# Two output transfers from two engines, and spare matmuls in TensorE's waits, in a decode kernel

## The chip, the cores and the metric

The kernel runs on one core of a Trainium2 chip. The metric is the device time of one execution in microseconds (us), as the median of several; "span" is the time from the first to the last instruction in a profiled execution, about 1.8 us shorter than the device time of the same execution (988.4 us in one of 990.19). An "issue" is the instruction by which an engine starts a transfer, a "landing" the moment at which the trace records that the transfer has completed. The change concerns the last 15 us of a run of 990 us.

## The reference

One decode step of a transformer block for 4 sequences of one token: layer norm, attention of 32 heads over caches of 4096 keys and values of width 192, an output projection with residual, then layer norm, a gated feed-forward part and a second residual.

```python
h  = x + attention(layernorm(x), k_cache, v_cache, wq) @ wo      # x: [4, 1, 640]
n  = layernorm(h)
h2 = h + (silu(n @ w_gate) * (n @ w_up)) @ w_down                # [640,1536], [640,1536], [1536,640]
```

The two caches are 403 MB of bfloat16. All weights together are about 22 MB. The output is 4 rows of 640 bfloat16 numbers, 5 KB.

## The kernel before

The kernel streams the caches through SBUF, and sends the weights of the last part behind them on the same queue. These are the parts that the change touches (cuts marked with `# ...`). `op` and `dma` note an instruction for an engine with the ones that it must wait for.

```python
    wd_land = {}
    for lo, hi in ((0, 6), (6, 11), (11, CF)):          # CF = 12 columns of w_down, in three transfers
        t = dma("sp", lambda e, lo=lo, hi=hi: e.dma_start(wdsb[:, lo:hi, :], ...), sem(f"s_wd{lo}"), k_free)
        for c in range(lo, hi):
            wd_land[c] = t
    # ... attention, wo ...
    ln2 = layer_norm(psH[:, 0:DQ], [wo_done])
    for k, w in enumerate((wgsb, wusb)):                # gate, then up
        for c in range(CD):                             # CD = 5
            for n in range(4):                          # four column tiles at a time, 384 columns each
                a = op("pe", lambda e, ...: e.matmul(PB[k][32 * n:32 * n + 32, 0:FQ], lhsT=lnT[:, c, :], ...),
                       [ln2, wu_land[c] if k else wg_land, ...])
        # ... silu on ScalarE after gate
    # ... gate times up, and its transpose, on VectorE
    for c in range(CF):
        for n in range(4):                              # 160 columns each
            a = op("pe", lambda e, c=c, n=n: e.matmul(psH[32 * n:32 * n + 32, 0:DQ], lhsT=guT[:, c, :], ...),
                   [gut, wd_land[c], ln2])
    a = op("dve", lambda e: e.tensor_copy(out=outsb[:, 0:DQ], in_=psH[:, 0:DQ]), [a])
    fin = dma("act", lambda e: e.dma_start(
        out[:, 0, :].rearrange("b (n d) -> n b d", n=4), outsb[0:128:RB, 0:DQ]), S_out, [a])
```

A result row of sequence `b` lies in four quarters, on partitions `32n + 8b`, so the output transfer writes 16 rows of 320 bytes in a 4 by 4 pattern. Matmuls come in groups of four that run side by side on the four column tiles of the array (in the trace of before, the first four of w_down start within 0.01 us).

## Time and profile before

| | before |
|---|---|
| device time, median of the 6 runs timed beside the changed kernel | 990.52 us (990.11 to 990.92) |
| span of the profiled run | 988.4 us |
| HBM read | 424.29 MB, 429 GB/s over the span |
| last landing of w_down | 985.08 us |
| copy of the result starts | 985.79 us |
| output issued / complete | 986.14 / 987.90 us |

The page of the kernel before: the share of DMA in 40 equal slices of the span (tenths), and the chain of work that ended last, by engine and by line.

```profile
span 988.4 us, 9461 instructions
...
DMA  9999999999999999999999999999999999999997
...
DMA 67%; PE 18%; DVE 12%; issue 1%; SPq 1%; DVEq 0%
```

All slices but the last have DMA at nine tenths or more. The chain is DMA for two thirds; the VectorE and TensorE pieces in it are the work that sets cache buffers free for the next load (SyncE's issues of the value loads waited for TensorE 30 times, 836.7 us in all). The change leaves that part alone. What it can shorten is the tail behind the last bytes of w_down.

The timeline of the tail: start, duration, engine, line, what is written and read, how often; in brackets the idle time of the engine before it and what ended it.

```profile
975.92 1.79 PE L563 MATMUL pb<-wg_sb,lnT 128*32 128x384 bf16 x20 [1.90 <-DVE lnT L322]
...
978.60 1.15 PE L563 MATMUL pb<-wu_sb,lnT 128*32 128x384 bf16 x12 [0.88 <-DMA wu_sb<-in_B_w_up_dram]
...
980.48 0.83 PE L563 MATMUL pb<-wu_sb,lnT 128*32 128x384 bf16 x8 [0.73 <-DMA wu_sb<-in_B_w_up_dram]
...
982.93 0.99 PE L573 MATMUL pb<-wd_sb,guT 128*32 128x160 bf16 x24 [1.62 <-DVE guT L569]
...
984.75 0.99 PE L573 MATMUL pb<-wd_sb,guT 128*32 128x160 bf16 x24 [0.83 <-DMA wd_sb<-in_B_w_down_dram]
985.79 0.33 DVE L576 CAST gu<-pb 128x160 bf16<-128x160 f32 x1 [2.91 <-PE pb L573]
986.14 1.13 ACTq L577 DMA_DIRECT2D out_dram<-gu  x1
```

TensorE waits for w_up twice (0.88 and 0.73 us), for VectorE's transpose (1.62), and for the second chunk of w_down (0.83). The last 24 matmuls start at 984.75, and the copy can start 1.04 us later. The output's issue is one instruction of ScalarE, 1.13 us long.

The chain of waits in order of time gives the release of those 24 matmuls (start, duration, what):

```profile
946.58 38.12 DMA wd_sb<-in_B_w_down_dram
...
984.75 1.02 PE pb L573 x18
...
985.79 0.33 DVE gu L576
```

The last w_down chunk landed at 985.08, by the landings that the trace records, but the matmuls that need it came last in the row of 24, and were not held up by it.

The granted clock, by windows (busy time of TensorE first; then weight loads, VectorE, ScalarE, GpSimd; the granted share of full clock; DMA share; GB/s):

```profile
core 0: us, PE busy (x) PEld busy (x) DVE busy (x) ACT busy (x) POOL busy (x), PEclk, DMA share, GB/s
975.40:978.80 3.40, 1.99 (x24) 0.84 (x28) 0.44 (x2) 1.20 (x2) 0.00 (x0) 0.50 1.00 413
978.80:982.20 3.40, 1.78 (x20) 0.29 (x12) 0.73 (x2) 0.00 (x0) 0.00 (x0) 0.50 1.01 413
...
984.70:985.80 1.10, 0.99 (x24) 0.67 (x24) 0.01 (x1) 0.00 (x0) 0.00 (x0) 0.50 0.00 0
```

From 975.4 us on TensorE has half its clock (0.50).

### The profile page before, as it was taken

The page shows a single profiled execution, that of the slowest core. Times are in us where ns is not written, and L with a number is a line of the kernel's source. Part 1 is how long each engine was busy: PE and PEld are TensorE (multiplying, and loading weights), DVE is VectorE, ACT ScalarE, POOL GpSimd, SP SyncE. Part 2 cuts the span into 40 slices and gives each one's busy share as a digit, 9 for nine tenths or more (in the row PEclk, how much of TensorE's full clock was granted, in tenths as well). Part 3 has the DMA queues.
Part 4 walks back from the last instruction along what each step waited for, and adds up shares of the span by engine and source line. Part 5 has one row for each costly group of instructions (what it writes and reads, how often), then busy time and mean ns, then how long its engine had stood idle before and what let it go on. Part 6 is the DMA issues. An engine that isn't in the chain of part 4 may idle for free.

```text
span 988.4 us, 9461 instructions
## 1 busy us (share of the span) xinstructions
PE 580.1 (59%) x4409; PEld 129.6 (13%) x2941; DVE 552.5 (56%) x447; ACT 117.1 (12%) x376; POOL 3.6 (0%) x18
## 2 busy tenths in 40 slices
PE   1677555666555576555557755656665555765554
PEld 0011011110101111001111110111101011110023
DVE  1486555566645556664556665555666455566621
ACT  0311111110111110011111011111101111100120
POOL 1000000000000000000000000000000000000000
PEclk9898777887777888777788777788877778887775
DMA  9999999999999999999999999999999999999997
GB/s 403 426 440 432 430 438 424 440 430 434 438 424 442 430 432 438 424 442 430 434 436 426 440 434 430 438 426 438 434 430 438 426 438 434 430 438 426 438 431 325
DMA packets 10571, 424.39 MB, mean 429 GB/s; under 512 B 1220, under 2 KB 1348, under 8 KB 1732
## 3 DMA queue, kind: packets, MB, share of 16 engines
q1 hardware_dynamic: 10512, 424.28, 99.5%
q8 instruction: 5, 0.08, 0.0%
q10 hardware_dynamic: 52, 0.01, 0.0%
q14 instruction: 2, 0.02, 0.0%
HBM read 424.29 MB, written 0.01 MB: 429 GB/s over the span
## 4 chain that ended last, share of the span: by engine, by line
DMA 67%; PE 18%; DVE 12%; issue 1%; SPq 1%; DVEq 0%
DMA k<-in_A_k_cache_dram 63%; DVE prod L413 12%; PE pb L161 12%; PE pb L463 4%; DMA wd_sb<-in_B_w_down_dram 4%; PE pb L421 2%; SPq L366 0%; DVE sc L426 0%; PE pb L469 0%; DVEq L413 0%; PE pb L573 0%; SPq L386 0%; SPq L392 0%; PE pb L435 0%; SPq L331 0%
## 5 line engine op out<-in xcount | busy, mean ns | idle before, releaser
L413 DVE TENSOR_TENSOR prod<-k,qball 128x6144 f16<-128x6144 bf16 x128 | 426.3, 3352 | 220.7 <-DMA k<-in_A_k_cache_dram 220.7
L161 PE MATMUL pb<-prod,identH 128*128 128x512 f16 x1408 | 385.0, 430 | 0.0
L421 PE MATMUL pb<-prod,identH 128*128 128x512 f16 x128 | 57.9, 452 | 339.5 <-DVE prod L413 339.5
L426 DVE TENSOR_REDUCE sc<-pb 128x32 f32<-128x512 f32 x128 | 88.0, 688 | 107.6 <-PE pb L161 107.6
L478 ACT ACTIVATE otmp<-pb,minv 128x192 f32<-128x192 f32 x32 | 13.5, 421 | 650.8 <-PE pb L463 650.8
L421 PEld LDWEIGHTS pb<-prod,identH 128*128 128x128 f16 x128 | 13.2, 103 | 586.2 <-DVE prod L413 481.3
L463 PE MATMUL pb<-v,pbuf 128*8 128x384 bf16 x1984 | 86.0, 326 | 0.0
L454 ACT ACTIVATE pbuf<-sc,negM 32x128 bf16<-32x128 f32 x128 | 73.4, 574 | 4.9
L463 PEld LDWEIGHTS pb<-v,pbuf 128*8 128x8 bf16 x1984 | 45.4, 86 | 28.8
L482 DVE SCALAR_TENSOR_TENSOR orow<-pb,minv,otmp 128x192 f32<-128x192 f32 x32 | 13.4, 418 | 55.0 <-ACT otmp L478 55.0
L498 PEld LDWEIGHTS pb<-orow,here 128*128 128x128 f32 x256 | 33.5, 191 | 73.8 <-issue 71.1
L498 PE MATMUL pb<-orow,here 128*128 128x48 f32 x256 | 31.7, 267 | 1.1 <-DVE orow L482 1.1
L454 ACT ACTIVATION_READ_ACCUMULATOR pbuf<-sc,negM 32x1 f32 x128 | 31.8, 248 | 0.0
L448 ACT ACTIVATE negM<-pb 128x4 f32<-128x4 f32 x32 | 5.6, 174 | 160.9 <-PE pb L444 160.9
L469 PEld LDWEIGHTS pb<-lsb,headm 128*128 128x128 f32 x64 | 12.3, 194 | 74.8 <-issue 71.1
L444 PE MATMUL pb<-negMc,ones_row 1*128 1x4 f32 x64 | 12.2, 258 | 11.9 <-DVE negMc L439 11.9
L435 PE MATMUL pb<-identF,msb 128*1 128x128 f32 x64 | 12.1, 271 | 9.8 <-DVE msb L431 9.8
L439 DVE TENSOR_REDUCE negMc<-pb 1x4 f32<-1x128 f32 x32 | 8.9, 279 | 15.1 <-PE pb L435 15.1
L444 PEld LDWEIGHTS pb<-negMc,ones_row 1*128 1x128 f32 x64 | 9.4, 182 | 21.3 <-DVE negMc L439 21.3
L469 PE MATMUL pb<-lsb,headm 128*128 128x1 f32 x64 | 9.2, 213 | 2.7 <-ACT pbuf L454 2.7
L491 ACT ACTIVATE here<-place 128x131 f32 (+1 forms) x32 | 10.0, 312 | 0.9
L431 DVE TENSOR_REDUCE msb<-sc 128x1 f32<-128x128 f32 x32 | 9.2, 286 | 1.1
(65 smaller groups left out, 85.1 us busy)
## 6 DMA issues: line engine op xcount, KB each, us to landing
k<-in_A_k_cache_dram SPq DMA_DIRECT2D x32, 6144.0 KB, 39.5
v<-in_A_v_cache_dram SPq DMA_DIRECT2D x31, 6144.0 KB, 25.5
wq_sb<-in_A_wq_dram SPq DMA_DIRECT2D x1, 7680.0 KB, 21.4
k<-in_A_v_cache_dram SPq DMA_DIRECT2D x1, 6144.0 KB, 39.2
wo_sb<-in_A_wo_dram SPq DMA_DIRECT2D x1, 5760.0 KB, 24.9
wo_sb<-in_A_wo_dram SPq DMA_DIRECT2D x1, 1920.0 KB, 26.9
wg_sb<-in_B_w_gate_dram SPq DMA_DIRECT2D x1, 1920.0 KB, 31.1
wu_sb<-in_B_w_up_dram SPq DMA_DIRECT2D x1, 1152.0 KB, 33.4
```

The source lines that it names most:

```text
L161: return e.add_instruction(mybir.InstMatmult(name=e.bass.get_next_instruction_name(), engine=mybir.EngineType.PE, start_tensor_calc=start, ...
L413: op("dve", lambda e: e.tensor_tensor(out=prod[BUF[k]][:, :, :], in0=kslot[u % 2][:, k * QT:(k + 1) * QT, :], in1=qball[:, bass.ds(u + pr. ...
L421: op("pe", lambda e, j=j: (e.matmul if j == 0 else partial(held_matmul, e))(psR[k][:, 0:QT * R], lhsT=identH[:, :], rhs=prod[BUF[k]][:, :, ...
L426: op("dve", lambda e: e.tensor_reduce(sc[u % 2][:, k * QT:(k + 1) * QT], psR[k][:, 0:QT * R].rearrange("q (t r) -> q t r", r=R), AX.X, ALU ...
L435: op("pe", lambda e: e.matmul(psS[0:1, XT], lhsT=msb[:, 0:1], rhs=identF[:, :], start=True, stop=True), [g("rmax", u), g("negM", u - 1), p ...
L444: op("pe", lambda e: e.matmul(psS[:, XB], lhsT=ones_row[0:1, :], rhs=negMc[0:1, :], start=True, stop=True), [g("hmax", u), g("negM", u - 1 ...
L454: op("act", lambda e, h=h, r=r: e.activation(out=pbuf[r, :, h], in_=sc[u % 2][r, :], func=ACTF.Exp, bias=negM[r, h:h + 1], scale=alpha, ac ...
L463: op("pe", lambda e, t=t, n=n: e.matmul(psO[32 * n:32 * n + 8, 0:2 * DH], lhsT=pbuf[:, t:t + 2, :].rearrange("q t m -> q (t m)"), rhs=vsrc ...
L469: op("pe", lambda e: e.matmul(psS[:, XL], lhsT=headm[:, :, :].rearrange("q r m -> q (r m)"), rhs=lsb[:, :], start=True, stop=True), [g("ex ...
L478: op("act", lambda e: e.activation(out=otmp[:, :], in_=psO[:, 0:DH], func=ACTF.Copy, scale=minv[:, 0:1]), [g("pv", u), g("minv", u), g("st ...
L482: op("dve", lambda e: e.scalar_tensor_tensor(out=orow[:, :], in0=psO[:, DH:2 * DH], scalar=minv[:, 1:2], in1=otmp[:, :], op0=ALU.mult, op1 ...
L498: op("pe", lambda e, i=i: e.matmul(psT[:, bass.ds(JW * at_unit(u)[0], JW)], lhsT=here[:, NI - 1 - i:NI - 1 - i + 128], rhs=orow[:, JW * i: ...
```

## The change

Three things are done, with the same arithmetic. The output goes in two transfers of eight rows, one from SyncE and one from ScalarE, so that each has half of the rows. Fourteen matmuls whose result nobody reads fill the waits of the feed-forward part, so that the clock comes up to full. And w_down arrives as 6, 4 and 2 columns instead of 6, 5 and 1, so that fewer matmuls are left behind its second chunk.

```diff
-    for lo, hi in ((0, 6), (6, 11), (11, CF)):
+    for lo, hi in ((0, 6), (6, 10), (10, CF)):
 # ...
+    def idle(n):
+        for _ in range(n):
+            op("pe", lambda e: e.matmul(PB[2][:, 0:256], lhsT=sel[:, 0, :], rhs=sel[:, 0:2, :].rearrange("q b m -> q (b m)"),
+                                        start=True, stop=True), [tk["rsum", NU - 1, NQ - 1]])
     for k, w in enumerate((wgsb, wusb)):
         for c in range(CD):
+            if c == 3 and k == 1:
+                idle(2)
 # ... gate / up matmuls
+        idle(6 if k else 3)
 # ...
     for c in range(CF):
+        if c == 6:
+            idle(3)
 # ... w_down matmuls, copy
-    fin = dma("act", lambda e: e.dma_start(
-        out[:, 0, :].rearrange("b (n d) -> n b d", n=4),
-outsb[0:128:RB, 0:DQ]), S_out, [a])
+    fin = [dma(eng, lambda e, n=n: e.dma_start(
+        out[:, 0, n * DQ:(n + 2) * DQ].rearrange("b (n d) -> n b d", n=2),
+        outsb[32 * n:32 * n + 64:RB, 0:DQ]), S_out, [a]) for n, eng in ((0, "sp"), (2, "act"))]
 # ...
-        pr.emit(block, "act", [fin])
+        pr.emit(block, "act", fin[-1:])
```

Both transfers raise the same semaphore, and ScalarE waits at the end for the sum of both.

## The prediction

> **What bounds it now.** DMA. The page's slices show the DMA share at nine tenths or more in all but the last, about 430 GB/s; the chain that ended last is 67% DMA. In the tail it is still the w_down load until 984.70 us, then the second half of the w_down matmuls (1.02 us), the copy (0.33), and the output: its issue on ScalarE is one instruction of 1.13 us (986.14 to 987.27) for 16 rows; completion is recorded at 987.90, the span closes at 988.4. Only these last 3.7 us can change; what comes before is set by 424 MB of reads that the change leaves alone.

> **What the change does.**
> 1. *w_down split 6/5/1 columns becomes 6/4/2.* Same bytes, so the last chunk should still land at 985.08 (issue at 947.07 plus 38.0). Before, the second chunk landed at 984.70 and 24 matmuls ran behind it; the last four needed the third chunk only at 985.25, so it was hidden. Now the second chunk should land near 984.3 (estimate: one column takes 55 ns a row, eight rows an engine), its 16 matmuls finish in the wait, and 8 run after 985.08. Groups of four start 0.133 us apart, the tail after the last start is 0.37: the copy is released near 985.6 instead of 985.76. Gain 0.15 us.
> 2. *14 spare matmuls of 256 columns.* Each costs about 0.21 us at half clock (estimate, from 0.133 for 160 columns). They fit the waits: before w_up (0.88 us idle, 0.64 used), within it (0.73; 0.43), after it (1.62; 1.28), within w_down (0.83; 0.64). They serve only the clock. Its record changes on a grid of 3.413 us[...]. In this trace half clock turned to full after a window that matmuls filled to 0.79 or more (34 cases), never at 0.76 or less. In the feed-forward part the shares were 0.53, 0.39, 0.46: half clock to the end. With the spares I work out 0.73, then 0.86: full clock from about 982.2. The last 8 matmuls then cost about 0.15 us less (a matmul took 0.233 us at full clock at the end of wo, 0.341 here). Earlier matmuls wait for DMA anyway. Chance that the clock is up in time: 80%.
> 3. *Output in two transfers of 8 rows.* The 1.13 us issue compares with 0.33 (after a wait) for a plain 128-row load, so part of it goes by rows or outer dimension; I take 0.8 for each half (0.55 to 1.13). [...] The closing wait covers both. Gain 0.2 us net.

> **Sum.** 0.15 + 0.12 + 0.2, about 0.5 us of 990.47: **989.95 us**, range 989.3 to 990.6 (before's runs spread 0.4). Faster by over 2%: 0.002; within 2%: 0.996; slower: 0.002.

> **What would show it.** Landings: second w_down chunk near 984.3, last near 985.1. Windows: full clock after about 982; 8 matmuls after the last landing, done 0.4 to 0.5 us later. Timeline: two output issues near 985.8, each under 0.9 us.

> **What would make it wrong.** The two issues exclude each other (no gain, or 0.3 us loss); 8 rows cost the same 1.1 us; a grid that falls so that no window reaches 0.79; a spare matmul delaying a real one; or landings that shift by tenths from run to run and hide it.

The sum stands as 0.15 + 0.12 + 0.2, 0.47 us. That the two issues would run side by side, on which the 0.2 rests, was the assumption; no trace of before shows it.

## The result

| | before | changed |
|---|---|---|
| median of 6 runs | 990.52 us (990.11 to 990.92) | 990.44 us (990.08 to 990.74) |
| ratio, 95% interval | | 0.9999 (0.9986 to 1.0012) |
| span of the profiled run | 988.4 us | 988.3 us |

All these runs were fast, within 1.5% of the fastest run of the kernel. A ratio here is the mean time of one kernel's fast runs over that of the other's of the same rounds, so it is not quite the ratio of the medians. The time lies in the forecast range, but the forecast gain of 0.5 us does not show: the medians differ by 0.08 us, the six runs of the changed kernel spread over 0.66 us, and the interval of the ratio is about 1.3 us to either side, so that these times can neither show such a gain nor exclude it. One has to read the traces to see what the change did.

The page after, the lines that answer to those of before:

```profile
DMA  9999999999999999999999999999999999999997
...
DMA 67%; PE 18%; DVE 12%; issue 1%; SPq 1%; DVEq 0%
```

The bulk is the same. The timeline of the tail:

```profile
975.98 1.79 PE L570 MATMUL pb<-wg_sb,lnT 128*32 128x384 bf16 x20 [1.90 <-DVE lnT L322]
...
977.71 0.82 PE L562 MATMUL pb<-sel 128*128 128x256 bf16 x3
...
980.45 0.51 PE L570 MATMUL pb<-wu_sb,lnT 128*32 128x384 bf16 x8 [0.71 <-DMA wu_sb<-in_B_w_up_dram]
...
980.89 0.83 PE L562 MATMUL pb<-sel 128*128 128x256 bf16 x6
...
982.90 0.60 PE L583 MATMUL pb<-wd_sb,guT 128*32 128x160 bf16 x24 [1.18 <-DMA wd_sb<-in_B_w_down_dram]
...
984.36 0.46 PE L583 MATMUL pb<-wd_sb,guT 128*32 128x160 bf16 x16 [0.42 <-DMA wd_sb<-in_B_w_down_dram]
...
985.11 0.32 PE L583 MATMUL pb<-wd_sb,guT 128*32 128x160 bf16 x8 [0.29 <-DMA wd_sb<-in_B_w_down_dram]
985.48 0.33 DVE L586 CAST gu<-pb 128x160 bf16<-128x160 f32 x1 [2.96 <-PE pb L583]
985.84 0.68 SPq L587 DMA_DIRECT2D out_dram<-gu  x1
985.84 1.38 ACTq L587 DMA_DIRECT2D out_dram<-gu  x1
```

The lines with `pb<-sel` are the spare matmuls. None of them delays a real one here: the w_up and w_down matmuls behind them still wait for DMA or start with its landing. The 24 first matmuls of w_down took 0.60 us instead of 0.99, which is the clock. The second chunk now releases 16 matmuls at 984.36 and the third releases 8 at 985.11. The copy starts at 985.48, 0.30 us sooner than before. Both output issues start at 985.84. SyncE's takes 0.68 us and ScalarE's 1.38 us: longer than the one issue of all 16 rows (1.13).

The end of the chain in order of time:

```profile
947.14 37.92 DMA wd_sb<-in_B_w_down_dram
...
985.11 0.35 PE pb L583 x8
...
985.48 0.33 DVE gu L586
```

The clock by windows, as above:

```profile
975.40:978.80 3.40, 2.78 (x27) 1.13 (x31) 0.49 (x2) 1.25 (x2) 0.00 (x0) 0.52 1.01 420
978.80:982.20 3.40, 2.20 (x28) 0.90 (x20) 1.08 (x2) 0.00 (x0) 0.00 (x0) 0.98 1.00 408
...
984.70:985.80 1.10, 0.44 (x16) 0.12 (x8) 0.32 (x1) 0.00 (x0) 0.00 (x0) 1.00 0.00 0
```

Full clock from 979.0 on. The chain now goes through the last chunk of w_down, as forecast.

When the rows really move is not in the timeline, which shows only the issue. Windows of 0.1 us show it in their last two columns, DMA share and GB/s. Before:

```profile
987.30:987.40 0.10, 0.00 (x0) 0.00 (x0) 0.00 (x0) 0.00 (x0) 0.00 (x0) 0.50 0.00 0
987.40:987.50 0.10, 0.00 (x0) 0.00 (x0) 0.00 (x0) 0.00 (x0) 0.00 (x0) 0.50 0.15 38
987.50:987.60 0.10, 0.00 (x0) 0.00 (x0) 0.00 (x0) 0.00 (x0) 0.00 (x0) 0.50 0.07 13
```

And after:

```profile
987.10:987.20 0.10, 0.00 (x0) 0.00 (x0) 0.00 (x0) 0.00 (x0) 0.00 (x0) 0.50 0.11 26
987.20:987.30 0.10, 0.00 (x0) 0.00 (x0) 0.00 (x0) 0.00 (x0) 0.00 (x0) 0.50 0.00 0
987.30:987.40 0.10, 0.00 (x0) 0.00 (x0) 0.00 (x0) 0.00 (x0) 0.00 (x0) 0.50 0.04 10
987.40:987.50 0.10, 0.00 (x0) 0.00 (x0) 0.00 (x0) 0.00 (x0) 0.00 (x0) 0.50 0.07 16
```

Before, all rows move between 987.4 and 987.6. After, there are two bursts, with nothing in 987.2 to 987.3. The trace's DMA packets say it to the nanosecond: the first half's rows start at 987.111 us and its last packet at 987.184, the second half's start at 987.380. So the DMA engines stood idle for almost 0.2 us before the second half: it was not held up by the moving of the first half's rows.

The tail of every run below, from the trace's own records (us). "Copy" and "rows" are the starts of the copy and of the first row's packet, "complete" is the last semaphore step of the output, "end" the end of the span. Landings differ by some tenths between runs, so each row is counted from its own last landing of w_down:

```
run                    last landing   copy     issue to  issue to   copy to    landing
                       of w_down      after it rows      complete   complete   to end
before                 985.075        0.711    1.289     1.758      2.116      3.299
changed                985.064        0.419    1.540*    1.962*     2.319      3.209
e1_act_half            985.030        0.552    1.292     1.718      2.074      3.097
e2_split_only          985.095        0.671    1.551*    1.976*     2.332      3.475
e3_one_output          985.078        0.418    1.294     1.770      2.127      3.017
e4_spares_only         984.958        0.350    1.298     1.766      2.122      2.943
e5_sp_one              985.106        0.677    1.298     1.764      2.117      3.257
e8_wd_only             985.146        0.553    1.286     1.758      2.116      3.141
e11_hold               984.884        0.349    1.293     1.766      2.122      2.943
e12_spares_again       984.886        0.351    1.297     1.760      2.117      2.940
* ScalarE's transfer, the later of two
```

So the account of the change is: copy 0.29 us sooner after the last landing (0.711 to 0.419), output 0.20 us slower (2.116 to 2.319), together 0.09 us (3.299 to 3.209). The first of these is good to some 0.04 us: in before, e2 and e5, which do the same up to the copy, the copy comes 0.671 to 0.711 us after the last landing, as it is the second chunk that releases the 24 matmuls there. The second is firmer: copy to complete is 2.116 to 2.127 us in all seven runs with one full transfer, and 2.319 and 2.332 with two.

### The profile page after: what moved, and what is told of

It is laid out like the page before. It is cut to its first block, busy times and chain, and to the rows that moved or that the text cites. A ratio compares the mean times of both kernels' runs of the same rounds, so it can differ in the third digit from the quotient of the medians.

```text
span 988.3 us, 9490 instructions
## 1 busy us (share of the span) xinstructions
PE 581.4 (59%) x4423; PEld 130.2 (13%) x2955; DVE 552.6 (56%) x447; ACT 117.1 (12%) x376; POOL 3.6 (0%) x18
## 4 chain that ended last, share of the span: by engine, by line
DMA 67%; PE 18%; DVE 12%; issue 1%; SPq 1%; DVEq 0%
DMA k<-in_A_k_cache_dram 63%; DVE prod L413 12%; PE pb L161 12%; PE pb L463 4%; DMA wd_sb<-in_B_w_down_dram 4%; PE pb L421 2%; SPq L366 0%; DVE sc L426 0%; PE pb L469 0%; DVEq L413 0%; SPq L392 0%; SPq L386 0%; PE pb L435 0%; SPq L331 0%; PE pb L583 0%
## 5 line engine op out<-in xcount | busy, mean ns | idle before, releaser
L505 PE MATMUL pb<-wo_sb,OT 128*32 128x160 bf16 x192 | 6.1, 323 | 6.2 <-DMA wo_sb<-in_A_wo_dram 6.2
```

## The experiments

Theory A at the start: the two issues exclude each other, so that the 1.38 us of ScalarE is SyncE's 0.68 plus 0.70 of its own. Rivals were that an issue on ScalarE is slow in itself, and that the clock or the spare matmuls disturb it. All runs below were compared with runs of the kernel before on the same chip. One of those runs of before took 1156.82 us; it is not used. The runs e1, e2 and e8 have one time each, so their state is unknown; they are read by the pieces of their tails.

### e1: ScalarE's half alone

```diff
-        ... for n, eng in ((0, "sp"), (2, "act"))]
+        ... for n, eng in ((2, "act"),)]
```

Half of the output is not written.

> The changed kernel without SyncE's transfer, so that half of the output is left unwritten (wrong on purpose). Theory A, the two issues exclude each other and ScalarE's record of 1.38 us is 0.68 of waiting for SyncE's plus 0.70 of its own: ScalarE's issue alone takes 0.65 to 0.75 us, and the span gets about 0.6 us shorter than the changed kernel's at the same landing. Rival B, an issue on ScalarE is slow in itself, or slowed by the shape of its half: it stays at 1.2 to 1.4 us.

Measured: the output's issue, from the view of that tile (shortest/median/longest in ns, start):

```profile
L587 ACTq DMA_DIRECT2D out_dram<-gu x1: 1134/1134/1134, 985.9 to 985.9; - x1
```

1134 ns for 8 rows, against 1129 for 16. Theory A's sum of 0.68 and 0.70 is wrong, and so is the premise under the change and under my forecast: halving the rows does not shorten ScalarE's issue at all. The rows still start 1.29 us after the issue's start. (The comparison of spans that was forecast is spoiled by the clock, which stayed at half in this run; see below. At half clock the last three spare matmuls also ran past the landing of the second w_down chunk, 984.25, and held its 16 matmuls up to 984.52. That cost nothing, as the third chunk came at 985.03: the copy started 0.552 us after it, as in e8 without any spare matmul, 0.553.) What the pair adds on ScalarE is 1.38 minus 1.13, 0.25 us.

### e2: the two transfers alone

The kernel before with only the last part of the change.

> The kernel before with the output in two transfers, nothing else. Theory A: the issue that comes second takes 1.35 to 1.40 us against 1.13 of the one transfer, so copy end to last completion grows from 1.78 us (986.12 to 987.90) to 1.95 to 2.05. The clock stays at half in the last 6 us, the last 24 matmuls take 1.0 us. Rival C, the 1.38 us comes from the full clock or the spare matmuls of the changed kernel: the issues are near 0.7 us both.

Measured: the issues, from the view of the output's tile:

```profile
L577 SPq DMA_DIRECT2D out_dram<-gu x1: 687/687/687, 986.1 to 986.1; - x1
L577 ACTq DMA_DIRECT2D out_dram<-gu x1: 1389/1389/1389, 986.1 to 986.1; - x1
```

SyncE's takes 687 ns and ScalarE's 1389, copy to completion is 2.33 us, with half clock and no spare matmuls. So neither the clock nor the spare matmuls make the second transfer late. From last landing to end 3.475 us, against 3.299 before: alone, this part of the change costs 0.18 us. (The copy to completion is 0.22 longer; the copy itself came 0.04 sooner after the landing.) As expected in size.

### e3: the changed kernel with one output transfer

The changed kernel with the output lines of the kernel before.

> The changed kernel with the one transfer of 16 rows of the kernel before. Theory A: issue 1.13 us again, completion 1.75 to 1.80 us after the copy; last w_down landing to span end 2.9 to 3.0 us, against 3.24 (988.3 minus 985.06) in the changed kernel and 3.3 before. The timed ratio cannot show 0.3 us (0.03%): same.

Measured: issue 1134 ns, completion 1.77 us after the issue's start, landing to end 3.017 us: 0.19 us less than in the changed kernel, just above the forecast 2.9 to 3.0. The timed ratio to before was 1.0002 (0.9985 to 1.0019), as forecast.

### e4 and e12: spare matmuls alone

The kernel before with the 14 spare matmuls, w_down in 6/5/1, one output transfer; run twice.

> The kernel before with the 14 spare matmuls only: w_down split 6/5/1, one transfer. If the clock is full at the end, the 20 matmuls of the second chunk run at 0.07 us a group of four and are done before the third lands near 985.05; the last four then end 0.28 us after it, which is as good as or 0.07 better than the 6/4/2 split. So the split of w_down is worth nothing once the clock is full. If the clock is at half, 24 matmuls take 1.0 us as before. Span 987.9 to 988.1 if the landings are where they were; timed: same.

> The kernel before with the 14 spare matmuls alone, a second time, for another position of the clock's grid and more rounds. If the grid allows a window of 0.79, the copy starts 0.35 us after the last landing again; if not, 0.70 as in the kernel before. Against the version that holds the clock: equal or up to 0.35 us slower.

Measured, e4: the clock went full at 983.72. The tail of its timeline:

```profile
984.60 0.66 PE L583 MATMUL pb<-wd_sb,guT 128*32 128x160 bf16 x24 [0.42 <-DMA wd_sb<-in_B_w_down_dram]
985.31 0.32 DVE L586 CAST gu<-pb 128x160 bf16<-128x160 f32 x1 [2.68 <-PE pb L583]
```

The copy starts 0.350 us after the last landing, against 0.419 with the 6/4/2 split at full clock and 0.711 before. So once the clock is full, the new split of w_down is 0.07 us worse than the old: with 6/5/1 only one group of four is left to wait for the last landing, with 6/4/2 two are. Landing to end 2.943 us. e12 had the full clock from 982.11 and gave the same, 0.351 and 2.940. Timed against before: 0.9996 (0.9979 to 1.0013) and 0.9998 (0.9984 to 1.0011). The medians were 0.56 and 0.35 us under those of before, which is the right direction, but the intervals do not resolve it.

### e8: the w_down split alone

```diff
-    for lo, hi in ((0, 6), (6, 11), (11, CF)):
+    for lo, hi in ((0, 6), (6, 10), (10, CF)):
```

> The kernel before with the w_down split 6/4/2 alone, clock at half at the end. My prediction's first step: second chunk near 984.3, last near 985.05, and the copy starts 0.54 us after the last landing instead of 0.71 (gain 0.15 to 0.19 us). The run without SyncE's half, whose clock stayed at half, had 0.55.

Measured: chunks landed at 984.384 and 985.146, the copy started 0.553 us after the last landing, 0.16 sooner than before. As forecast. So at half clock the split pays, and at full clock (e3 and e4) it costs: the two gains do not add.

### e5: the one output transfer from SyncE

```diff
-    fin = dma("act", lambda e: e.dma_start(
+    fin = dma("sp", lambda e: e.dma_start(
```

e1 suggested a new theory: the issue goes by the engine, and SyncE's is shorter. Then simply moving the output should gain 0.43 us.

> The kernel before with its one output transfer of 16 rows issued by SyncE instead of ScalarE, nothing else. The run without SyncE's half showed ScalarE's issue of 8 rows at 1.134 us, as long as its issue of 16 rows (1.129), while SyncE's 8 rows took 0.68. Theory D: the issue's length goes by the engine that issues and not by the rows. Then SyncE's issue of 16 rows takes 0.65 to 0.75 us and copy start to completion falls from 2.12 to about 1.65 to 1.70 us. Rival E, rows do count on SyncE: 0.9 to 1.2 us.

Measured: the issue, from the view of the output's tile:

```profile
L577 SPq DMA_DIRECT2D out_dram<-gu x1: 696/696/696, 986.1 to 986.1; - x1
```

And the windows in which the rows begin to move:

```profile
987.30:987.40 0.10, 0.00 (x0) 0.00 (x0) 0.00 (x0) 0.00 (x0) 0.00 (x0) 0.50 0.00 0
987.40:987.50 0.10, 0.00 (x0) 0.00 (x0) 0.00 (x0) 0.00 (x0) 0.00 (x0) 0.50 0.15 38
```

The issue is 0.43 us shorter, as theory D says, and it is worth nothing: the rows start 1.298 us after the issue's start, where they started 1.289 after ScalarE's, and copy to completion is 2.117 against 2.116 us. The forecast of 1.65 to 1.70 failed. Timed: 990.17 us against 990.56 of before, ratio 0.9998 (0.998 to 1.0015). So the recorded length of an issue is not the time to its first byte. ScalarE's extra 0.43 us runs beside the transfer's start, which takes 1.29 us either way. The data moves after the record: it ended 0.16 us before the first row on ScalarE (987.273 and 987.433, before) and 0.60 us before it on SyncE (986.832 and 987.434). What makes ScalarE's record longer, no run here shows.

### e6, e7, e9: the output 32 times over

One trace's 0.2 us could be chance, and no total can show it. So the output was written 32 times, each round after the last had landed: in one transfer from ScalarE (e6), in the changed kernel's two from two engines (e7), and in two from ScalarE (e9).

```diff
+    fin = [a]
+    for _ in range(32):
+        fin = [dma(eng, lambda e, n=n: e.dma_start(
+            out[:, 0, n * DQ:(n + 2) * DQ].rearrange("b (n d) -> n b d", n=2),
+            outsb[32 * n:32 * n + 64:RB, 0:DQ]), S_out, fin) for n, eng in ((0, "sp"), (2, "act"))]   # e7
```

> The kernel before with the output written 32 times over, each round one transfer of 16 rows from ScalarE, issued when the one before has landed. Theory D1, ScalarE always takes 1.13 us: all 32 issues at 1.1 to 1.15, a round of about 1.7 to 1.8 us, 31 rounds add 53 to 56 us. Theory D2, only the first issue after a long pause is slow: the later ones at 0.35 to 0.75 us, a round of 1.0 to 1.4 us, 31 rounds add 31 to 43 us.

> As the 32-fold single transfer, but each round in the changed kernel's two transfers from SyncE and ScalarE, the next round when both have landed. If the two issues shut each other out in part (1.38 against 1.13 us in the changed kernel), a round is 0.2 to 0.3 us longer than with one transfer, and 31 rounds take 6 to 9 us more (0.6 to 0.9%), clear of the noise. If the excess was a chance of one trace, the two kernels are within 1 us of each other, or the two-transfer one is shorter.

> As the 32-fold output in two transfers, but both from ScalarE, one issue after the other. The second issue cannot start before the first has ended, about 0.52 us later. Theory F, [...] a round is 0.4 to 0.6 us longer than with one transfer (1.68 us), against 0.22 from two engines. Rival G, [...] then it does not matter who issues, and a round is 0.2 to 0.3 us longer.

What is left to test is whether a round gets longer when one engine issues both transfers (F) or takes as long as with two (G).

The issues in the view of the output's tile (shortest/median/longest in ns, first and last start), e6:

```profile
L579 ACTq DMA_DIRECT2D out_dram<-gu x32: 543/543/1129, 986.1 to 1038.3; - x32
```

e7, SyncE and ScalarE:

```profile
L579 SPq DMA_DIRECT2D out_dram<-gu x32: 497/510/674, 986.1 to 1045.0; - x32
L579 ACTq DMA_DIRECT2D out_dram<-gu x32: 518/518/1377, 986.2 to 1045.1; - x32
```

e9:

```profile
L579 ACTq DMA_DIRECT2D out_dram<-gu x64: 517/518/1134, 986.1 to 1053.9; - x64
```

| | one transfer (e6) | two, two engines (e7) | two, ScalarE (e9) |
|---|---|---|---|
| median time | 1042.36 us | 1049.46 us | 1058.05 us |
| a round, mean of 31 in the trace | 1.683 us | 1.900 us | 2.170 us |
| added per round over e6, from the medians over 32 rounds | | 0.22 us | 0.49 us |

The 4 runs of each spread by less than 0.8 us, so here the totals do tell. Two engines cost 0.22 us a round more than one transfer, 7.1 us in all: the loss is real. As to e6: of 32 issues only the first takes 1129 ns, all others 543, so the long one is the first of them only (as in theory D2; whether the pause before it makes it long, or the other work of ScalarE in between, these runs do not part). Yet a round takes 1.68 us, where D2 expected 1.0 to 1.4 from the shorter issues: again the issue's length hardly enters. From the trace's packets, the rows start 1.19 us after a later issue's start and 1.29 after the first.

e9 has the length that theory F forecast (0.4 to 0.6 us a round) and not G's (0.2 to 0.3), but it does not show what delays the second of two transfers that two engines issue at once. Its second issue starts 0.55 us after its first, and the second half's rows start 1.16 us after their own issue, as the first half's do: all of its delay is the wait for ScalarE's first issue to end, and a delay of G's size would be over by then. Nor is it the moving of the first half's rows that delays the second: in e7's 31 later rounds the second half's rows start 0.27 to 0.36 us behind the first's, and no packet of either half moves in the last 0.18 to 0.28 us of that. The landings record two completion steps for each half (changed) and four for the whole transfer (before), beside one step for each transfer 0.04 to 0.08 us before its first row; what that says of how the rows are divided, no run here tests. A round is 0.49 us longer when one engine issues both one after the other, and 0.22 when two engines issue at once.

These rounds also show that the longer record is not the delay. In e7 ScalarE's issue is recorded at 1377 ns in the first round and at 518 or 519 in all others, as long as in e9, where nothing is issued beside it (519); the second half's rows are 0.27 us or more behind in every round. Two engines save 0.27 of the 0.49 us a round that the second transfer costs when one engine issues both. They do not make it free: 0.22 us a round is left.

### e10: a plain pattern

One transfer 32 times over, the output side as one stretch of 16 rows (the rows come out in another order, wrong).

> The 32-fold single transfer from ScalarE, with the rows written in another order (wrong on purpose), so that the output side is one plain stretch of 16 rows of 320 bytes in place of a 4 by 4 pattern. If the pattern is what costs between issue and first packet (1.29 us), the issue falls to 0.33 to 0.45 us and a round from 1.68 to 1.2 to 1.5 us. If it is a fixed time of any transfer, a round stays within 0.1 us of 1.68 though the issue's record gets shorter, as it did when SyncE issued.

Measured: issue 592 ns the first time, then 501 (543 with the pattern); 16 completion steps a transfer in place of 4; a round 1.736 us, 0.05 longer than e6; median 1043.92 us. The first issue lost 0.54 us of its recorded length, and the round gained nothing. So the 4 by 4 pattern is not what the output's time goes to, and rearranging the output for a plain pattern was not tried.

### e11: a version that should hold the clock

In e1, with the very spare matmuls of the changed kernel, the clock stayed at half. The clock changes on a grid of 3.413 us that falls differently in each run (full clock began at 978.97 us in changed, 982.11 in e12, 983.72 in e4). The matmuls of wo had full clock at their end (in before from 972.0 us on, 0.233 us a matmul against 0.341). So spare matmuls were also put into the layer norm that follows (32 in all, in place of 14), to hold the clock instead of raising it again; with 6/5/1 and one output transfer.

```diff
+    idle(6)
     ln2 = layer_norm(psH[:, 0:DQ], [wo_done])
+    idle(8)
 # ... and 4, 3, 8, 3 instead of 3, 2, 6, 3
```

> A version meant to beat both kernels: one output transfer from ScalarE, w_down split 6/5/1 as before, spare matmuls in the feed-forward part (4, 3, 8, 3) and 14 more in the layer norm that follows wo (6 before its matmul, 8 after), so that the full clock that wo reaches is never lost. If a window of 3.413 us that matmuls fill to 0.38 or more holds the full clock (as every such window of the kernel before did), the clock stays full from wo to the end whatever the grid; the copy starts 0.33 to 0.38 us after the last landing and the span ends 2.9 to 3.0 us after it (before 3.30, changed 3.21). The run without SyncE's half, with the changed kernel's spares, had missed the full clock. If the clock drops, 24 matmuls at half clock: 3.3. Timed: same, some 0.3 us or 0.03% lower, which the rounds will hardly resolve.

Measured, the clock by windows:

```profile
975.40:978.80 3.40, 1.96 (x36) 0.98 (x36) 0.79 (x2) 1.55 (x2) 0.00 (x0) 1.00 1.00 413
978.80:982.20 3.40, 2.17 (x27) 1.03 (x19) 1.29 (x2) 0.00 (x0) 0.00 (x0) 1.00 1.00 408
...
984.70:985.80 1.10, 0.48 (x24) 0.25 (x15) 0.32 (x1) 0.00 (x0) 0.00 (x0) 1.00 0.00 0
```

And the end of its timeline:

```profile
984.52 0.66 PE L585 MATMUL pb<-wd_sb,guT 128*32 128x160 bf16 x24 [0.83 <-DMA wd_sb<-in_B_w_down_dram]
985.23 0.32 DVE L588 CAST gu<-pb 128x160 bf16<-128x160 f32 x1 [2.92 <-PE pb L585]
```

Full clock from 972.19 to 985.84. The copy starts 0.349 us after the last landing, landing to end is 2.943 us, 0.36 less than before: as forecast. (The gate matmuls began some 0.5 us later than in e12, at 976.28 against 975.74 with the same landings, as the layer norm's matmul had come late, at 974.10 against 973.46; w_up, which lands at 978.33, was still to come.) Timed: 990.06 us, median of 5, against 990.50 of before; ratio 0.9998 (0.9985 to 1.0012). It equals e12, whose clock came up in time with 14 spare matmuls. That it holds the clock at every position of the grid is argued and not shown: one profile has one position.

### The clock, over all traces

```
run                first windows of the part: share filled -> clock of the next window
before             0.53 -> half   0.39 -> half   0.46 -> half
changed            0.76 -> full   0.43 -> full   0.35 -> half (after the last matmul)
e1_act_half        0.58 -> half   0.72 -> half   0.46 -> half
e3_one_output      0.81 -> full   0.41 -> full   0.35 -> half (after the last matmul)
e4_spares_only     0.44 -> half   0.77 -> full   0.21 -> half (after the last matmul)
e12_spares_again   0.74 -> half   0.80 -> full   0.39 -> full
```

With the 14 spare matmuls the clock was full for the last matmuls in four runs of five.

## Why the prediction was right or wrong

The time, 990.44 us, lies within 989.3 to 990.6 and within 2% of before, as forecast; with a spread of runs of 0.7 us this says little, and before itself (990.52) lies in that range. That the time agrees is no sign that the steps were right. By steps:

1. *What bounds the kernel.* Right. DMA is in the chain until the last landing (985.08 before, 985.06 after), and the last landing did not move.
2. *The w_down split, 0.15 us.* Right at the clock for which it was worked out: the second chunk landed at 984.32 (forecast 984.3), the last at 985.06 (985.08), and alone it gave 0.16 us (e8). But its worth depends on the clock, which the forecast missed: with the old split and full clock the copy starts 0.07 us sooner than with the new (0.350 and 0.419).
3. *The spare matmuls.* Right in mechanism. The share of the first window came out at 0.76 instead of 0.73 and was enough, so the clock rose at 978.97 and not at 982.2. That was luck: by the forecast's own rule (0.79 raises it, 0.76 never did) this window would not have done it; e12, with 0.74 and then 0.80, took the course that was forecast. Split and clock together were forecast at 0.30 us once the clock is up (0.15 each; the sum has 0.12 for the second, for its chance of 80%) and gave 0.29. The chance of 80% for the clock stands beside four runs of five. I missed that the spare matmuls alone give 0.36.
4. *The output.* Wrong, and this is the step that failed: "so part of it goes by rows or outer dimension; I take 0.8 for each half ... Gain 0.2 us net." The 1.13 us had been set against 0.33 us of a load that SyncE issues, another engine and another pattern. ScalarE's issue of half the rows takes as long as that of all (1.134 and 1.129 us, e1). And the completion does not follow the issue's recorded length anyway: SyncE's is 0.43 us shorter, with the same completion (e5). What the output takes is about 1.29 us from issue to first row, whoever issues, about 0.13 us of rows and some 0.35 us until the completion is seen; two transfers pay the start once each, and the second's comes 0.27 us behind the first's. In place of a gain of 0.2 there was a loss of 0.20, and in place of two issues "each under 0.9 us" ScalarE's of 1.38. The text named the outcome in its last paragraph ("the two issues exclude each other (no gain, or 0.3 us loss)"), but the reason given there is only half right: the second transfer is held up before its rows move, by what is open, and the first saves next to nothing in exchange (its rows start 1.276 us after its issue, where those of the whole start after 1.289).

The sum of 0.5 us was thus 0.29 minus 0.20, 0.09 us in the profiled tail.

What stays open is what holds the second transfer up. In every run with two issuers ScalarE issued some 5 ns after SyncE; the order was not reversed, so it is also open whether the later issuer waits or ScalarE's transfer does. The DMA engines' idle time before the second burst (0.19 us in changed, 0.18 to 0.28 in e7's later rounds) places it before the data moves, between issue and first packet. In changed ScalarE's record is 0.25 us longer beside SyncE's, and its rows are 0.27 us behind; but in e7's later rounds the record does not grow (518 ns) and the rows are still 0.27 us or more behind, so what lengthens the record does not account for those. Also open is why ScalarE's first issue of the output is recorded at 1.13 us and the later ones at 0.54 (with the plain pattern of e10, 0.59 and 0.50).

## What to carry to other kernels

Time a small transfer from its issue to its first packet and to its completion before trying to shorten it: the issue's length in the timeline is not its cost (on SyncE it was 0.43 us shorter and the completion the same), and cutting 16 rows into two transfers only added a second start here (0.20 us in the tail, 0.22 us a round). Spare matmuls that bring the clock up are worth having where a few real matmuls stand between the last landing and the end (here they alone gave 0.36 us), but count how much of each clock window they fill (in the ten traces here 0.78 was enough every time, 0.75 never). Holding a full clock that was there already took about as many columns in a window as raising it (0.37 and 0.39 of a full window); e11 did it with 32 spare matmuls and ended no sooner than e12, which raised it with 14. What holding may gain is that it depends less on where the windows fall, which the one profile of e11 does not show. When the effect is smaller than the spread of the runs, repeat the disputed piece 32 times, and judge the parts from the trace.
